# Spectral filter and two MLPs on one core: conversions, folds, mixing's weight parts and last low parts given other places

## Chip, core and metric

The kernel runs on one core of one Trainium2 chip. The metric is the device time of the program in microseconds (us) on that core, as the median of three runs. Durations of single instructions and stages come from one profiled execution of the program.

Engines are named as in the profile: PE is TensorE's matmuls and PEld its weight loads, DVE is VectorE, ACT is ScalarE, POOL is GpSimd, SP is SyncE, which issues the loads. A line number such as L865 is a line of the kernel's file.

## The reference

What is computed: a real FFT along the sequence, a complex 256x256 mixing with bias and a soft threshold, the inverse FFT, and then two MLPs of width 2048. The weights come in float64, x in float32.

```python
# x: (2, 3008, 256)
X = np.fft.rfft(x, axis=1)
Yr = Xr @ w_r - Xi @ w_i + b_r
Yi = Xr @ w_i + Xi @ w_r + b_i
Yr = np.sign(Yr) * np.maximum(np.abs(Yr) - 0.01, 0.0)      # Yi the same
y = np.fft.irfft(Yr + 1j * Yi, n=3008, axis=1)
# twice, on 6016 tokens, with w_in (256, 2048), w_out (2048, 256)
h = x @ w_in
g = h * (1.0 / (1.0 + np.exp(-1.702 * h)))                 # second MLP: 1.0 for 1.702
x = g @ w_out
```

## The kernel before

**Stages.** The transforms are matmuls with constant matrices. All regions have a hand-written order: an engine runs its instructions as the Python code issues them, and an instruction whose input or buffer isn't ready holds up everything behind it on that engine.

*Forward.* Sixteen groups (q, b, t): q is the half of the samples, b the batch, t the kind of output. Symmetric samples are folded first on VectorE. `halves` (L308) makes half-sums of a loaded tile, and `one` folds them once more, with L340, and for some pairs with L349, into the tiles xf. `fold(g)` does both for a group, and runs three groups ahead of its matmuls (L384, L398, L416). `fwd_evac` empties the banks of the group before: copies on ScalarE (L441, L445), and sums and differences on VectorE (L431, called from L451 to L457).

*Mixing.* Twelve units (b, p, j), the "mids", of 25 matmuls each from the third on (L565 and one of bias, L568) and 9 before (L562). From the third mid on, a float32 product is three matmuls of a high and a low part: hi·hi, hi·lo, lo·hi. Data: xh is a copy on ScalarE (L504); xl is made by a ScalarE product with -1 (L500) and a DMA that adds x to it (L501), issued on POOL's queue. Weights: wh is a ScalarE copy (L546), wl a VectorE difference (L547). `mid_post` (L575 to L586) and `mid_fold` (L598 to L605) do bias threshold and folds behind the matmuls, one mid late.

*Inverse.* Sixteen steps: matmuls at L384 (out of `inv_mm`), `inv_post` (L690 to L715, the differences again at L431), `inv_out` (L745 to L749). Its results yt stay on the chip.

*MLPs.* Six blocks of 1024 tokens (the last has 896), each with eight groups, and a group is a pair of column chunks of w_in. `group` forms its products X, Y, Z at L865 by a scheme with seven instead of eight block products: copies on ScalarE at L884, L900, L902, sums on VectorE at L886, L910, L913. The gate is two ScalarE steps, the activation L868 and the cast L870 of its high part; L875 makes the low part, on POOL or VectorE. The second product (L837) takes the gate's parts one group late (`out_next`). `hook(h)` is called at six places in a group, and adds other work there.

**Weight conversion.** Float64 weights arrive as pairs of 32-bit words in one buffer, raw64 (one buffer, loads issued by SP at L162, L163 or L166). A conversion is: L175 on ScalarE, which writes the tile cv_c (one buffer); five VectorE steps L180 to L184, which `pump` takes out of the list `fill`; and L185, an accumulating DMA on POOL's queue that adds cv_c to the tile cv_a, followed by the load of the next raw. `place_in` and `place_out` then split cv_a into high and low parts: sums L213 to L216 on VectorE, high parts L109 on ScalarE, low parts L110 on POOL or VectorE, or in mode "D" (L105 to L107) by the accumulating DMA. `tick` (forward) and `window(1, ())` (mixing, inverse, MLP) start a conversion.

Where they start is in CFG: 'tf' lists forward groups, 'tm' mids, 'ti' steps of the inverse. In the first MLP block 'kb' gives the number for each group. The conversions of its groups 0, 1 and 2 are called A, B and C here (parts out 3, 4 and 5); the next one is D. A sits at hook 4 of group 0, the others at hook 1 of their group. Hook 3 of the group after places what was converted, through `window(0, done, True)`.

Within a group the hooks stand in this order on ScalarE:

```python
884        nc.scalar.copy(y1, X)
887        hook(1)
893            g11 = gate(0, 0, y1)
900        nc.scalar.copy(y2, Z)
902        nc.scalar.copy(y3, X)
905        hook(3)
911        g22 = gate(1, 1, y2)
915        g12 = gate(0, 1, y3)
917        hook(4)
922        rest(nc.gpsimd, *gate(1, 0, y4, X))
```

(Hook 2 stands between L893 and L900.) The two lines of the hook that the change touches are L989 and L990.

Of the kernel before, what the change touches and what calls it, by code (L numbers as in the profile page):

```python
# [56 lines left out]
def spectral_mlp_kernel(ctx, tc, xin, mfwd, minv, wc, bias, w_in1, w_out1, w_in2, w_out2, outT):  # L57
# [4 lines left out]
    def N(k):  # L62
        return CFG.get(k, NUM[k])
# [1089 lines left out]
```

## Time and profile before

| what | us | share of the span |
|---|---|---|
| median of three runs (1172.51 to 1173.91) | 1173.24 | |
| profiled execution, its time | 1174.34 | |
| profiled execution, span | 1172.5 | |
| TensorE busy | 1150.7 | 98% |
| ScalarE busy | 772.5 | 66% |
| VectorE busy | 634.6 | 54% |
| POOL busy | 490.5 | 42% |
| moved by DMA | 66.65 MB | |

The mean granted clock of TensorE is 0.997 of full speed (full is 2.4 GHz). The span runs from the first to the last recorded instruction; the program's time has some 2 us more around it. Busy shares are means over stages: a share near 100% says that an engine can hardly be given less idle time, not that it never waits. The forward stage takes up the first 65 us, mixing goes on to about 133, the inverse to 185, and the rest is the two MLPs.

### The profile page before, as it was taken

How to read it: one execution, taken by the hardware profiler on the slowest of the kernel's cores; microseconds unless marked ns; L12 is line 12 of the kernel's file. 1: busy time of each engine (PE TensorE's matmuls, PEld its weight loads, DVE VectorE, ACT ScalarE, POOL GpSimd, SP SyncE). 2: the span in 40 equal slices, each digit the busy share in tenths (PEclk: the TensorE clock that was granted, in tenths of full speed). 3: DMA queues.
4: the chain of work that ended last, by engine and by line, in shares of the span. 5: the costliest groups of instructions: out<-in, count | busy, mean ns of one | idle time of the engine just before them, and what ended most of it. 6: DMA issues, size and time to landing. Idle time of an engine off the chain costs nothing.

```text
span 1172.5 us, 14601 instructions
## 1 busy us (share of the span) xinstructions
PE 1150.7 (98%) x5086; PEld 948.0 (81%) x5086; DVE 634.6 (54%) x1001; ACT 772.5 (66%) x1440; POOL 490.5 (42%) x418
## 2 busy tenths in 40 slices
PE   9999997999999999999999999999999999999998
PEld 6767865777888888888889978888888888888897
DVE  7778895676457465574573552442532623523522
ACT  2467455768667667677677776676766765866755
POOL 0255353444444444444446755343333333433333
PEclk9999999899999999999999999999999999999999
DMA  8566785421221121121220100010000000000000
GB/s 294 162 115 128 205 132 107 108 55 37 72 63 34 48 72 37 36 72 37 63 63 19 55 19 18 0 37 1 1 37 1 18 19 1 37 1 1 36 1 32
DMA packets 38268, 66.65 MB, mean 57 GB/s; under 512 B 3505, under 2 KB 15153, under 8 KB 38194
## 3 DMA queue, kind: packets, MB, share of 16 engines
q1 hardware_dynamic: 26306, 45.90, 11.9%
q0 software_dynamic: 11888, 19.82, 9.8%
q8 instruction: 40, 0.66, 0.2%
q14 instruction: 34, 0.28, 0.1%
HBM read 35.53 MB, written 10.35 MB: 39 GB/s over the span
## 4 chain that ended last, share of the span: by engine, by line
PE 81%; DVE 6%; ACT 4%; DMA 4%; issue 3%; POOL 1%; SPq 0%; DVEq 0%; ACTq 0%; POOLq 0%
PE o L837 40%; PE x L865 36%; PE psi L384 3%; DMA cv_a<-cv_c 2%; ACT yt L868 1%; DMA xl<-xt 1%; PE psf L384 1%; PE psf L416 1%; DMA raw<-in_x 1%; DVE cv_a L182 1%; ACT xh L504 0%; ACT xl L500 0%; DMA xr<-in_x 0%; ACT x L774 0%; ACT yt L884 0%
## 5 line engine op out<-in xcount | busy, mean ns | idle before, releaser
L875 POOL TENSOR_TENSOR g<-yt,g 128x512 fp32r<-128x512 f32 (+1 forms) x282 | 363.0, 1299 | 497.8 <-PE x L865 320.6
L837 PE MATMUL o<-g,wo 128*128 128x512 f32 (+1 forms) x2304 | 561.4, 386 | 0.6 <-DMA wo<-cv_a 0.6
L865 PE MATMUL x<-x,wi 128*128 128x512 f32 (+1 forms) x2016 | 500.8, 387 | 11.5 <-ACT yt L902 9.3
L837 PEld LDWEIGHTS o<-g,wo 128*128 128x128 f32 x2304 | 433.3, 188 | 82.0 <-DMA wo<-cv_a 1.0
L865 PEld LDWEIGHTS x<-x,wi 128*128 128x128 f32 x2016 | 377.6, 188 | 90.0 <-ACT yt L902 12.8
L868 ACT ACTIVATE yt<-yt 128x512 f32<-128x512 f32 (+1 forms) x288 | 179.2, 622 | 255.2 <-DVE yt L910 206.2
L870 ACT CAST g<-yt 128x512 fp32r<-128x512 f32 (+1 forms) x384 | 235.2, 612 | 12.2
L910 DVE TENSOR_TENSOR yt<-yt,x 128x512 f32<-128x512 f32 (+1 forms) x96 | 64.8, 675 | 217.5 <-PE x L865 216.9
L886 DVE TENSOR_TENSOR yt<-yt,x 128x512 f32<-128x512 f32 (+1 forms) x96 | 64.9, 676 | 166.7 <-ACT yt L884 166.4
L875 DVE TENSOR_TENSOR g<-yt,g 128x512 fp32r<-128x512 f32 (+1 forms) x102 | 70.2, 688 | 71.9 <-ACT g L870 71.0
L185 POOL DMA_DIRECT2D cv_a<-cv_c x32 | 28.1, 877 | 121.1 <-DVE cv_c L184 94.4
L913 DVE TENSOR_TENSOR yt<-yt,x 128x512 f32<-128x512 f32 (+1 forms) x96 | 64.8, 675 | 0.6 <-PE x L865 0.6
L781 DVE TENSOR_TENSOR x<-yt,x 128x512 fp32r<-128x512 f32 (+1 forms) x44 | 46.1, 1049 | 29.7 <-ACT x L774 29.7
L868 ACT ACTIVATE yt<-x 128x512 f32<-128x512 f32 (+1 forms) x96 | 56.1, 584 | 1.3 <-PE x L865 1.3
L884 ACT COPY yt<-x 128x512 f32<-128x512 f32 (+1 forms) x96 | 54.7, 570 | 2.4 <-issue 2.4
L902 ACT COPY yt<-x 128x512 f32<-128x512 f32 (+1 forms) x96 | 55.7, 580 | 0.1
L900 ACT COPY yt<-x 128x512 f32<-128x512 f32 (+1 forms) x96 | 54.8, 571 | 0.8 <-PE x L865 0.8
L384 PE MATMUL psi<-m,f 128*128 128x376 f32 (+3 forms) x208 | 50.2, 396 | 1.0 <-DVE rt L431 1.0
L384 PEld LDWEIGHTS psi<-m,f 128*128 128x128 f32 x208 | 36.5, 190 | 13.2 <-DVE rt L431 1.6
L175 ACT ACTIVATE cv_c<-raw 128x512 f32<-128x512 f32 x32 | 21.5, 673 | 22.6 <-DMA cv_a<-cv_c 18.2
L384 PE MATMUL psf<-m,xf 128*128 128x190 f32 (+2 forms) x176 | 36.1, 366 | 0.0
L565 PE MATMUL psm<-wh,xl 128*128 128x512 f32 x88 | 34.6, 393 | 1.1 <-DMA xl<-xt 1.0
(123 smaller groups left out, 853.5 us busy)
## 6 DMA issues: line engine op xcount, KB each, us to landing
raw<-in_wi SPq DMA_DIRECT2D x32, 256.0 KB, 3.6
cv_a<-cv_c POOLq DMA_DIRECT2D x32, 256.0 KB, 5.0
raw<-in_wo SPq DMA_DIRECT2D x16, 512.0 KB, 3.9
xl<-xt POOLq DMA_DIRECT2D x22, 256.0 KB, 5.5
out_t<-yt SPq DMA_DIRECT2D x20, 256.0 KB, 2.1
raw<-in_x SPq DMA_DIRECT2D x9, 512.0 KB, 5.6
m<-in_mi SPq DMA_DIRECT2D x4, 564.0 KB, 8.8
w_in<-cv_a SPq DMA_DIRECT2D x8, 256.0 KB, 2.0
```

Source lines behind the costliest of these rows:

```text
L384: nc.tensor.matmul(ps, hi[:, c : c + P], m[:, k, :w], start=i == 0, stop=i == last)
L837: nc.tensor.matmul(acc[h, mm], st, mv, start=first and k == 0, stop=last and k == 2)
L865: nc.tensor.matmul(ps, st, mv, start=first and m == 0, stop=m == 2, skip_group_check=True)
L868: nc.scalar.activation(g, g if src is None else src, func)
L870: nc.scalar.copy(gh, g)
L875: eng.tensor_sub(gl, g, r32(gh))
L884: nc.scalar.copy(y1, X)
L886: nc.vector.tensor_add(y1, y1, Y)
L900: nc.scalar.copy(y2, Z)
L902: nc.scalar.copy(y3, X)
L910: nc.vector.tensor_add(y2, y2, X)
L913: nc.vector.tensor_add(y3, y3, Z)
```

## The change

Seven edits, all of order, place or engine; the arithmetic is the same.

1. Forward: the third conversion tick goes from group 13 to group 14 ('tf').
2. Mixing: conversions start at mids 2, 5, 8, 10 instead of 1, 4, 7, 10 ('tm').
3. Inverse: the low parts L110 of weight part 4 go from VectorE to POOL.
4. `fold`: for groups with t = 0 behind the first, each half-sum is followed at once by the fold that reads it, instead of all half-sums first.
5. `xsplit`: the low parts of the last mid are made by POOL (tensor_sub) right behind their high parts, instead of a ScalarE product and an accumulating DMA each.
6. Start of mixing: wh and wl are issued ahead of the last `fwd_evac`.
7. MLP: B goes from hook 1 to hook 4 of group 1, C from hook 1 to hook 2 of group 2; A and the later ones stay.

```diff
--- before.py
+++ after.py
@@ -8,7 +8,7 @@
 
-CFG = {
...
-'tf': [6, 10, 13], 'tm': [1, 4, 7, 10],
...
+CFG = {
...
+'tf': [6, 10, 14], 'tm': [2, 5, 8, 10],
...
 
@@ -247,7 +247,7 @@
     def window(k, done, now=False):
         for u, a in done:
             if u[0] == "in":
-                sums, puts = place_in(u[1], u[2], a, (nc.vector if u[2] == NPR // 2 else "D") if modes[0] else E('pil', u[2]), sums_tmp)
+                sums, puts = place_in(u[1], u[2], a, (nc.gpsimd if u[2] == NPR // 2 else "D") if modes[0] else E('pil', u[2]), sums_tmp)
                 if now:
                     for f in (puts[0], *sums, puts[1]):
                         f()
@@ -313,12 +313,10 @@
         q, b, t = groups[g]
 
         cs, pair = t % 2, []
-        if t == 0 and g:
-            for j in range(NJ):
+        for j in range(NJ):
+            if t == 0:
                 halves(q, b, j, 0)
-        for j in range(NJ):
             if g == 0:
-                halves(q, b, j, 0)
                 one(0, j, pair)
                 halves(q, b, j, 1)
                 load_raw()
@@ -493,6 +491,8 @@
             return
         b, p, j = mids[i]
         k = (i - N('n32')) % 4
+        if part and i == len(mids) - 1:
+            return
         for cs in range(2):
             x = xt[b, p, j, cs].rearrange("p q m c -> p (q m c)")
             if part:
@@ -502,6 +502,10 @@
             else:
                 t = lo_p[1].tile([P, 512], F32R, tag="hi", name="xh")
                 nc.scalar.copy(t, x)
+                if i == len(mids) - 1:
+                    lo = lo_p[bool(k)].tile([P, 512], F32R, tag="lo", name="xl", bufs=6 if k else 2)
+                    nc.gpsimd.tensor_sub(lo, x, r32(t))
+                    xsp[b, p, j, cs, 1] = lo[:, :].rearrange("p (q m c) -> p q m c", q=2, m=2)
             xsp[b, p, j, cs, part] = t[:, :].rearrange("p (q m c) -> p q m c", q=2, m=2)
 
     first = fwd_first()
@@ -542,9 +546,9 @@
     lo_p.append(opened("nh", "left", N('nhb')))
     wh = wh_p.tile([P, 2, 3 * D], F32R, name="wh")
     wl = wh_p.tile([P, 2, 3 * D], F32R, name="wl")
-    fwd_evac(*prev)
     nc.scalar.copy(wh, wc_s)
     nc.vector.tensor_sub(wl, wc_s, r32(wh))
+    fwd_evac(*prev)
 
     def mid_mm(i):
         b, p, j = mids[i]
@@ -986,7 +990,7 @@
             if h == 3:
                 window(0, done, True)
                 done[:] = []
-            if h == (1 if at else 4):
+            if h == {0: 4, 1: 4, 2: 2}.get(at, 1):
                 window(k, ())
             if h in (2, 3):
                 moved(h)
```

## Rows read from the trace of the kernel before

**Rows 1.** TensorE's waits, whole span: us in total, times, longest.
```profile
PE x L865 <- ACT yt L902: 9.3, 8, 6.3
PE psf L416 <- DVE xf L340: 1.7, 1, 1.7
...
PE psm L565 <- DMA xl<-xt: 1.0, 1, 1.0
```

**Rows 2.** timeline of TensorE, MLP's groups 1 and 2: start, us, instruction [idle <-releaser].
```profile
196.77 2.92 PE L837 MATMUL o<-g,wo 128*128 128x512 f32 x12
205.95 2.93 PE L865 MATMUL x<-x,wi 128*128 128x512 f32 x6 [6.26 <-ACT yt L902]
...
211.24 2.27 PE L865 MATMUL x<-x,wi 128*128 128x512 f32 x9
```

**Rows 3.** stretches: length, busy us of PE, PEld, DVE, ACT, POOL; PEclk, DMA, GB/s.
```profile
199.00:204.50 5.50, 0.69 (x4) 0.23 (x2) 0.68 (x2) 1.37 (x3) 1.23 (x1) 1.00 0.57 140
204.50:206.00 1.50, 0.05 (x1) 0.05 (x1) 1.40 (x4) 1.40 (x3) 0.00 (x0) 0.50 0.00 0
300.00:400.00 100.00, 99.76 (x441) 82.27 (x440) 56.36 (x78) 67.76 (x120) 42.16 (x34) 1.00 0.19 50
```

**Rows 4.** timeline of ScalarE, MLP's groups 0 and 1: conversions A and B.
```profile
193.62 0.66 ACT L175 ACTIVATE cv_c<-raw 128x512 f32<-128x512 f32 x1
...
203.10 0.66 ACT L175 ACTIVATE cv_c<-raw 128x512 f32<-128x512 f32 x1 [7.20 <-DMA cv_a<-cv_c]
```

**Rows 5.** line L185, stretches 193:200, 105:106, 112:120 and 236:240.
```profile
DMA to landing us min/median/max: 5.0/5.0/5.0
...
DMA to landing us min/median/max: 4.5/4.5/4.5
...
L185 POOL DMA_DIRECT2D cv_a<-cv_c x1: 877/877/877, 117.1 to 117.1; - x1
...
DMA to landing us min/median/max: 8.4/8.4/8.4
...
DMA to landing us min/median/max: 6.1/6.1/6.1
```

**Rows 6.** timeline of VectorE, MLP's group 1.
```profile
197.66 0.68 DVE L886 TENSOR_TENSOR yt<-yt,x 128x512 f32<-128x512 f32 x1
```

**Rows 7.** page, costliest groups: busy us, mean ns of one, idle before, releaser.
```profile
L868 ACT ACTIVATE yt<-yt 128x512 f32<-128x512 f32 (+1 forms) x288 | 179.2, 622 | 255.2 <-DVE yt L910 206.2
...
L902 ACT COPY yt<-x 128x512 f32<-128x512 f32 (+1 forms) x96 | 55.7, 580 | 0.1
```

**Rows 8.** timeline of VectorE, forward stage.
```profile
15.08 0.69 DVE L308 TENSOR_TENSOR keep<-xr 128x512 f32<-128x512 f32 x1 [0.59 <-DMA xr<-in_x]
...
26.39 2.43 DVE L340 TENSOR_TENSOR xf<-lv 128x256 f32<-128x256 f32 x7
...
32.77 0.76 DVE L349 TENSOR_TENSOR xf<-dd 128x256 f32<-128x256 f32 x2 [0.51 <-PE psf L384]
...
37.91 0.43 DVE L181 TENSOR_SCALAR cv_c<-cv_c 128x512 uint32<-128x512 uint32 x1
```

**Rows 9.** timeline of ScalarE, start of mixing.
```profile
65.00 0.47 ACT L445 COPY eo<-psf 128x376 f32<-128x376 f32 x1 [4.09 <-DVE xt L431]
```

**Rows 10.** timeline of TensorE, start of mixing.
```profile
67.42 0.50 PE L565 MATMUL psm<-wh,xh 128*128 128x512 f32 x1 [0.22 <-ACT xh L504]
68.69 0.50 PE L565 MATMUL psm<-wl,xh 128*128 128x512 f32 x1 [0.78 <-DVE wl L547]
```

**Rows 11.** timeline of VectorE, end of mixing and inverse.
```profile
148.66 0.55 DVE L110 TENSOR_TENSOR wi<-cv_a,wi 128x384 fp32r<-128x384 f32 x1
...
156.68 0.55 DVE L431 TENSOR_TENSOR rt<-psi,eo 128x376 f32<-128x376 f32 x1
```

**Rows 12.** timeline of ScalarE, mid 10.
```profile
125.52 0.67 ACT L175 ACTIVATE cv_c<-raw 128x512 f32<-128x512 f32 x1 [1.03 <-DMA cv_a<-cv_c]
```

**Rows 13.** timeline of VectorE, last ticks of the forward stage.
```profile
59.88 1.11 DVE L181 TENSOR_SCALAR cv_c<-cv_c 128x512 uint32<-128x512 uint32 x1
```

More of the change, by code (lines that the diff above doesn't have):

```diff
@@ L10 @@
 F32 = mybir.dt.float32
-CFG = {'lv0': 'V', 'lv': 'V', 'dd0': 'VPVVPPPPPVVP', 'dd': 'V', 'ths': 'VVVVPV', 'thf': 'VVVP', 'ivf': 'V', 'cva': 'P', 'pol': 'PPPP', 'pil': 'P', 'mvl': 'PVVP', 'xl': 'V', 'xse': 'V', 'gl': 'VPPPPPPP', 'tf': [6, 10, 13], 'tm': [1, 4, 7, 10], 'ml': [], 'pk': 6, 'ti': [3, 7], 'pi': 4, 'pl': [1, 4, 8, 10, 13], 'kb': [1, 1, 1, 1, 1, 1, 1, 0], 'kr': [0, 1, 0, 1, 0, 1, 1, 0], 'fa': 3, 'xp': [2, 4, 4, 5], 'xq': [1, 4, 1], 'xs': 4, 'xi': [7, 7, 9, 10, 10, 11, 8], 'xsi': 9, 'xo': (0, 1, 6, 2, 3, 4, 5), 'xd': (0, 1, 4, 6), 'ca': 4, 'tl': True, 'fwd': 'all', 'rest0': 'all', 'rest1': 'all', 'last1': 'all', 'inv': 'all', 'mid': 'all', 'last0': 'all', 'thm': 'A', 'gl0': 'PVPVVVPV', 'gl2': 'PPPPPPPP', 'gl3': 'PPPPPPPV', 'xl0': 'V', 'xl1': 'V', 'pre': 14, 'pre2': 0, 'yd': 6, 'lvb': 6, 'mlp': 'all', 'pr': 'V', 'pf': 'PV', 'eo': '0110', 'n32': 1, 'li': [8, 10, 11], 'lii': [0], 'xa': 4, 'nhb': 6, 'ddb': 6, 'mlp1': 'all', 'mlp2': 'all'}
+CFG = {'lv0': 'V', 'lv': 'V', 'dd0': 'VPVVPPPPPVVP', 'dd': 'V', 'ths': 'VVVVPV', 'thf': 'VVVP', 'ivf': 'V', 'cva': 'P', 'pol': 'PPPP', 'pil': 'P', 'mvl': 'PVVP', 'xl': 'V', 'xse': 'V', 'gl': 'VPPPPPPP', 'tf': [6, 10, 14], 'tm': [2, 5, 8, 10], 'ml': [], 'pk': 6, 'ti': [3, 7], 'pi': 4, 'pl': [1, 4, 8, 10, 13], 'kb': [1, 1, 1, 1, 1, 1, 1, 0], 'kr': [0, 1, 0, 1, 0, 1, 1, 0], 'fa': 3, 'xp': [2, 4, 4, 5], 'xq': [1, 4, 1], 'xs': 4, 'xi': [7, 7, 9, 10, 10, 11, 8], 'xsi': 9, 'xo': (0, 1, 6, 2, 3, 4, 5), 'xd': (0, 1, 4, 6), 'ca': 4, 'tl': True, 'fwd': 'all', 'rest0': 'all', 'rest1': 'all', 'last1': 'all', 'inv': 'all', 'mid': 'all', 'last0': 'all', 'thm': 'A', 'gl0': 'PVPVVVPV', 'gl2': 'PPPPPPPP', 'gl3': 'PPPPPPPV', 'xl0': 'V', 'xl1': 'V', 'pre': 14, 'pre2': 0, 'yd': 6, 'lvb': 6, 'mlp': 'all', 'pr': 'V', 'pf': 'PV', 'eo': '0110', 'n32': 1, 'li': [8, 10, 11], 'lii': [0], 'xa': 4, 'nhb': 6, 'ddb': 6, 'mlp1': 'all', 'mlp2': 'all'}
 NUM = dict(li=[5, 6, 7, 8], n32=2, pk=4, ydp=2, lii=[1, 3], xd=(), ml=[], pl=[], xo=range(7), pi=6, nhb=6, tf=[5, 9, 13], tm=[1, 3, 5, 7, 9, 11], ti=[0, 2, 4, 6, 8, 10, 12, 14, 14, 15, 15], kb=[2] * 8, kr=1, fa=3, fe=2, pm=0, nf=4, lvb=6, ddb=8, ivb=1, eob=1, fsb=6, f1=3, f2=0, fm=[7, 8, 9], fi=[1, 1, 2, 2], pre=13, pre2=1, yd=3, psh=0, ie=[12], xp=[1, 3, 4, 5], xq=[1, 2, 2], xs=5, nw=4, xi=[14, 14, 15, 15], xsi=13, rw=2, ca=4, cc=2, tb=1, tmn=1)
```

## The prediction

> **What bounds the kernel now.** Three views, in this order. The page's busy shares (the table above) give TensorE 98% of the span: moving work can win only what TensorE waits for, or runs at a lower clock. TensorE's waits [rows 1] then name the places: one of 6.3 us in the MLP, for the copy L902, one of 1.7 in the forward fold (xf) and one of 1.0 at the end of mixing (xl). Each lies in a stage that the change touches. Last the timelines around the long one. TensorE ends its work at 199.69 (196.77 + 2.92) and goes on at 205.95 [rows 2]. The granted clock is full until 204.5 and half, 1.2 GHz, after it [rows 3]: the 12 matmuls from 205.95 to 211.24 take 5.29 us [rows 2]. In a steady stretch one follows the other by 100 / 441 = 0.227 us [rows 3], so twelve would take 2.7. The place costs 6.3 + 2.5 = 8.8 us.
>
> Its cause stands in ScalarE's queue [rows 4]. Conversion A's L175 runs at 193.62; behind the copy L884 of group 1 comes conversion B's L175 (hook 1 of group 1). It writes cv_c, of which there is one, and A's accumulating transfer still reads it: B's L175 waits 7.20 us, to 203.10, and the gate, L900 and L902 queue behind it. From one L175 to the next takes 203.10 - 193.62 = 9.5 us at the least, 5.0 of it the transfer [rows 5].
>
> **MLP: B to hook 4 of group 1, C to hook 2 of group 2.** In group 1 no transfer is waited for any more. L886 still stands on VectorE behind A's five steps and starts at 197.66 [rows 6]; 0.7 for it, 1.2 for the gate (L868 and a cast of the same size) and 1.2 for L900 and L902 [rows 7] bring L902's end to 200.7, and TensorE, ready at about 199.4, waits 1.3. From there two matmul groups, L910 and two gates (0.7 + 0.6 + 2.4, [rows 6, 7]) put B's L175 at 204.4, after A has landed: no wait. But between hook 4 of group 1 and hook 2 of group 2 ScalarE has only a gate, L884 and a gate (about 3.5 us), and the turn-round is 9.5. C's L175 can't start before 213.8; L900 and L902 behind it end at 215.4. TensorE, 45 matmuls (10.2 us at 0.227) after 200.4, wants L902 at 210.6: it waits 4.8 us there. So the wait is not gone, it stands one group later: 1.3 + 4.8 against 6.3 us. B and C are now placed together in group 3 (two more ScalarE casts in one hook, 1.1 us), and the last matmuls of group 2 come late behind the gates: 0.7 more. D follows C by nearly a whole group, so its wait is covered. Idle time then gets 0.6 us worse, and what is won is the half clock, 2.5 us, if it stays full over 4.8 us. In the old wait it fell at 204.5, 4.8 us after the last matmul; I take it that it just stays: **-1.9 us**. If it falls, +0.6. Were the wait gone altogether, 8.8 - 2.0 = 6.8 us would be won: the lower end.
>
> **The fold.** For groups with t = 0 each half-sum is now followed by its fold. In group 2 the half-sums come one by one with their loads, the last of them at 15.08 [rows 8]. So the first folds fill these gaps instead of standing behind 15.08, and the 1.7 us wait goes. It comes back: TensorE is next late for group 5, whose last fold (26.39) closes a VectorE row without a gap since 15.08. Two folds of 0.35 (2.43 / 7) taken out of that row, and some 0.5 of bubbles between dependent steps added, leave 0.15 us. In group 8 the order hurts: the fold at 32.77 waits 0.51 us for TensorE [rows 8], and now a half-sum (0.6) that used to be ahead of it stands behind. The conversion that follows on VectorE comes 0.6 us later, and with it the chain of transfers to mixing.
>
> **Start of mixing.** The conversion tick goes from group 13 to 14, and wh, wl ahead of the last evacuation. The tick itself doesn't move, since its L175 waited for a landing; but VectorE now evacuates group 13 before it. L445 waited 4.09 us for that, at 65.00 [rows 9], and wh stood behind it. Now wh stands right behind the copy of group 14, at about 61. ScalarE, which then runs without a gap for some 10 us, carries 4.0 us into the stage, and wl comes some 2 us earlier. TensorE's matmul for wl starts 68.69 - 67.42 = 1.27 after the one ahead of it [rows 10], 1.0 more than 0.227; the shorter wait ahead (0.22) and slow restarts make it some 1.5, by estimate, and all of it goes.
>
> **Mixing, and who gains from it.** The four conversions go from mids 1, 4, 7, 10 to 2, 5, 8, 10; the low parts of the last mid go from ScalarE and two transfers to POOL, 1.3 us each. The stall for xl (a wait of 1.0 [rows 1], 1.5 with restarts, taken from the place of wl) goes too, and TensorE could leave mixing 3.0 us early. It can't keep that: banks for the second half of the inverse are freed by VectorE's L431 at 156.68 [rows 11], and from mid 10's L175 (125.52, which waits for the third conversion's landing) [rows 12] VectorE has next to no gap up to there. That landing decides. Its transfer, issued at 117.1, took 8.4 us [rows 5]. Now: 117.1 - 4.0 (start) + 0.6 (fold) + 5.7 (one mid later: 25 matmuls at 0.227) = 119.4. How long it takes there no row shows: 4.5 at the least, 8.4 at the most [rows 5]. I take 5.5, near the short end, as the two transfers for xl that followed it are gone and two of four matrix loads no longer fall on it. It lands at 124.9, 0.6 before 125.5; by the ends, 1.6 before or 2.3 after.
>
> **Weight part 4 to POOL.** VectorE loses two L110 of 0.55 from 148.66 on [rows 11], 1.1 us in that row. POOL is idle there but for issues. A VectorE step beside a POOL L110 stretches: L181 took 1.11 us instead of 0.43 [rows 8, 13]. The first new POOL step falls on the sums L213 to L216, I put 0.3 on that; the second falls on L714 and L715, which read PSUM. Gain 0.8, between -0.2 and 1.1. The Trainium skill (SBUF — State Buffer, section "SBUF: two separate sides") says that a GpSimd operation and a VectorE operation with two SBUF inputs take a port pair in turns, each for its whole length. L181 agrees. If that held for every step beside the two, the gain would be gone and the time some 0.8 us more.
>
> L431 so comes 0.6 + 0.8 = 1.4 us earlier, and TensorE with it: **-1.4 us**, of 3.0 that it could have had; behind it TensorE is bound by its own matmuls up to the MLP. With the ends: 2.7 won, or 2.5 lost (2.3 late, 0.2 lost).
>
> **Sum.** The profiled execution has a span of 1172.5 and a time of 1174.34; the median is 1173.24. The differences are worked out on the span and taken off the median: 1173.24 - 1.4 - 1.9 = 1169.9.
>
> **Rivals.** (a) The clock falls again in the 4.8 us wait of group 2: price 2.5, 1172.4, within 0.2%. For it speaks that the rows show the fall at just that length of idling. The Trainium skill (TensorE: Matmul & The Clock Gate, section "HAM oscillation — how this bites in real kernels") warns that idle gaps put the array back to half clock, again and again in one kernel; by that rule 1172.4 is the result. Against it: one fall is all that the rows hold, and the new wait is no longer than the idling that came before it.
> (b) TensorE keeps what it wins in mixing, because the landing is quick and VectorE keeps up: 1173.24 - 3.0 - 1.9 = 1168.3. Against it: the gapless row on VectorE.
> (c) The wait in group 2 is hidden: 1173.24 - 1.4 - 6.8 = 1165.0. It would need a turn-round of under 5 us, where 9.5 is the shortest seen.
> (d) Slower: accumulating transfers land late where other loads run beside them. In mixing, 8.4 us puts L431 1.5 later (2.3 - 0.8). In the MLP 6.1 instead of 5.0 (which another of block 0 took [rows 5]) makes the wait of group 2 5.9 and takes the clock with it: +1.7. Together 1176.4. It decides from about 7 us in mixing; before, a landing of 8.4 came with four matrix loads and two xl transfers, now half of that.
> (e) That an edit does nothing, as for the tick of group 14: covered by (a), 1172.4.
>
> **How the numbers follow.** Forecast 46%, (a) with (e) 27%, (b) 12%, (c) 4%, (d) 11%. The range leaves out (c) and most of (d): 1166.6 to 1174.2. A measurement of this kernel can tell about 0.2% (2.3 us) from no change, that is 1170.9 and 1175.6. The forecast's cases lie below 1170.9 mostly (0.40 of 0.46), (b) and (c) wholly; (a) is the same but for 0.02; of (d) 0.09 is slower: faster 0.58, same 0.33, slower 0.09.
>
> **What would show it.** Right: a wait of TensorE for L902 of about 4.8 us in group 2 (near 209 to 214) and one of about 1.3 in group 1, at a full clock; no wait for xf in group 2 but small ones up to group 5; no waits for wl and xl; a wait of 1.5 to 3 us in the first half of the inverse for L431, and TensorE at the MLP's first matmul 1 to 2 us earlier than before. Wrong: half clock after the new wait; ScalarE at mid 10 waiting more than 3 us for the landing; the first MLP matmul 3 us earlier or more, which would say that VectorE doesn't bound the inverse.

## Result and profile after

The changed kernel takes 1179.16 us (median of 5 runs, 1178.32 to 1180.14) where the kernel before takes 1173.37 beside it: a ratio of 1.0051, 95% interval 1.0037 to 1.0066. It is slower by 6 us, and the forecast had it 3.3 us faster. Its profiled execution has a time of 1179.16 and a span of 1177.4, against 1172.5 before. One execution each of three kernels below took far longer (e7 3906.59, e9 3792.0, e10 1278.03 us) and is left out of medians and ratios.

Code ahead of `xsplit` stands 2 lines higher in the changed kernel, and code behind it 4 lines lower: L902 is now L906, L865 is L869, L837 is L841, L565 is L569, L579 is L583, L431 is L429, L340 is L338. L500 and L504 keep their numbers.

Where the time went is first seen by stage, one profiled execution of each kernel. The table has the starts of TensorE's first matmul of mixing (psm), of the inverse (psi) and of the MLPs (x), from the timelines of both kernels, and the distances between them.

| | mixing starts | inverse starts | MLPs start | mixing | inverse | MLPs to the last matmul's start |
|---|---|---|---|---|---|---|
| before | 59.93 | 133.58 | 185.52 | 73.65 | 51.94 | 982.85 |
| after | 60.36 | 135.68 | 191.84 | 75.32 | 56.16 | 981.40 |

Mixing lost 1.7 us and the inverse 4.2; the MLPs are 1.4 shorter. So what the forecast had from the stages ahead of the MLP (-1.4) came with the other sign, at +5.9. The MLPs' 1.4 looks like most of the forecast (-1.9), but kernels with the same MLP code differ by as much from profile to profile (see e3).

TensorE's waits of the changed kernel (us in total, times, longest) name what is new there:

```profile
PE x L869 <- ACT yt L906: 8.7, 9, 4.6
PE psm L569 <- ACT xh L504: 2.9, 2, 2.0
PE psi L382 <- DVE rt L429: 2.7, 2, 1.5
PE psi L382 <- DVE sd L583: 1.8, 1, 1.8
```

Against [rows 1]: the waits of 1.7 for xf and 1.0 for xl's transfer are gone, as forecast, but mixing now waits 2.9 us for xh, which before was late by 0.2 at the most [rows 10], and the inverse 1.8 for sd and 2.7 for rt (before, 1.0 for rt). Who holds up xh stands in ScalarE's timeline (start, us, instruction, [idle before <-releaser]):

```profile
112.05 1.39 ACT L587 ACTIVATE th<-sd,neglam 128x512 f32<-128x512 f32 x2 [4.53 <-DVE sd L581]
...
118.18 0.66 ACT L175 ACTIVATE cv_c<-raw 128x512 f32<-128x512 f32 x1 [3.71 <-DMA cv_a<-cv_c]
...
121.37 1.12 ACT L504 CAST xh<-xt 128x512 fp32r<-128x512 f32 x2
...
132.61 0.67 ACT L175 ACTIVATE cv_c<-raw 128x512 f32<-128x512 f32 x1 [3.75 <-DMA cv_a<-cv_c]
```

The first of the two waits for xh (0.9, at 112.7) comes from VectorE: its five steps of the second conversion (107.4 to 110.1) keep sd late, and L587 ahead of xh waits 4.53 for that. The second (2.04, at 119.6) comes from L175: the third conversion's (mid 8) waits 3.71 us for the second's transfer, and xh, at 121.37, stands behind it. The fourth's (mid 10) waits 3.75 us for the third's transfer, and starts at 132.61, 7.1 us later than its counterpart of [rows 12]. The accumulating transfers they wait for, line L185 in the stretches 110:112 and 125:126:

```profile
L185 POOL DMA_DIRECT2D cv_a<-cv_c x1: 877/877/877, 110.8 to 110.8; - x1
...
DMA to landing us min/median/max: 7.4/7.4/7.4
...
L185 POOL DMA_DIRECT2D cv_a<-cv_c x1: 877/877/877, 125.2 to 125.2; - x1
...
DMA to landing us min/median/max: 7.4/7.4/7.4
```

Both take 7.4 us. Before, the second conversion's transfer, of 105.4, took 4.5 [rows 5].

The clock falls twice. Stretches of the changed kernel (columns as in [rows 3]):

```profile
122.00:123.00 1.00, 0.98 (x4) 0.85 (x5) 0.93 (x3) 0.97 (x2) 0.00 (x0) 0.97 0.00 0
123.00:126.00 3.00, 3.00 (x8) 2.35 (x8) 2.93 (x6) 0.00 (x0) 0.85 (x2) 0.50 0.10 11
126.00:127.00 1.00, 1.00 (x5) 0.78 (x5) 1.00 (x4) 0.56 (x1) 1.00 (x2) 0.83 0.80 252
222.00:225.00 3.00, 2.90 (x7) 2.33 (x8) 2.90 (x6) 1.08 (x3) 0.78 (x2) 0.50 0.00 0
225.00:226.00 1.00, 1.00 (x6) 0.78 (x5) 0.96 (x2) 0.60 (x1) 0.98 (x2) 0.83 0.95 228
```

The half clock from just before 123 to 126.3 follows the 2.0 us wait for xh and makes mixing some 1.7 us longer; the other follows the new wait in the MLP:

```profile
207.00 1.66 PE L869 MATMUL x<-x,wi 128*128 128x512 f32 x6 [1.04 <-ACT yt L906]
...
214.63 2.88 PE L841 MATMUL o<-g,wo 128*128 128x512 f32 x12
222.10 2.93 PE L869 MATMUL x<-x,wi 128*128 128x512 f32 x6 [4.58 <-ACT yt L906]
```

That is rival (a)'s fall, after a wait of 4.58 us (forecast: 4.8) behind one of 1.04 in group 1 (forecast: 1.3).

### The profile page after: what moved, and what is told of

Its sections match the earlier page's. It is cut to its first block, busy times and chain, and to the rows that moved or that the text cites. A ratio compares the mean times of both kernels' runs of the same rounds, so it can differ in the third digit from the quotient of the medians.

```text
span 1177.4 us, 14595 instructions
## 1 busy us (share of the span) xinstructions
PE 1152.0 (98%) x5086; PEld 948.7 (81%) x5086; DVE 636.8 (54%) x999; ACT 772.3 (66%) x1438; POOL 494.1 (42%) x420
## 4 chain that ended last, share of the span: by engine, by line
PE 77%; DVE 5%; ACT 3%; issue 3%; DMA 1%; POOL 1%; DVEq 0%; POOLq 0%; ACTq 0%
PE o L841 39%; PE x L869 35%; PE psi L382 3%; ACT yt L872 1%; DMA cv_a<-cv_c 1%; DVE yt L890 0%; DVE cv_a L182 0%; ACT x L778 0%; ACT yt L888 0%; DVE th L590 0%; ACT g L874 0%; DVE cv_c L180 0%; DVE yt L914 0%; DVE tmp L213 0%; POOL g L879 0%
## 5 line engine op out<-in xcount | busy, mean ns | idle before, releaser
L841 PE MATMUL o<-g,wo 128*128 128x512 f32 (+1 forms) x2304 | 560.3, 385 | 0.5 <-DMA wo<-cv_a 0.5
L869 PE MATMUL x<-x,wi 128*128 128x512 f32 (+1 forms) x2016 | 500.8, 387 | 10.9 <-ACT yt L906 8.7
L841 PEld LDWEIGHTS o<-g,wo 128*128 128x128 f32 x2304 | 432.8, 188 | 81.7 <-DMA wo<-cv_a 1.0
L869 PEld LDWEIGHTS x<-x,wi 128*128 128x128 f32 x2016 | 377.3, 188 | 89.7 <-ACT yt L906 12.7
L914 DVE TENSOR_TENSOR yt<-yt,x 128x512 f32<-128x512 f32 (+1 forms) x96 | 64.8, 675 | 217.1 <-PE x L869 216.7
L185 POOL DMA_DIRECT2D cv_a<-cv_c x32 | 28.1, 878 | 125.4 <-DVE cv_c L184 93.0
L906 ACT COPY yt<-x 128x512 f32<-128x512 f32 (+1 forms) x96 | 55.8, 582 | 0.1
L569 PE MATMUL psm<-wh,xh 128*128 128x512 f32 x88 | 35.5, 404 | 2.9 <-ACT xh L504 2.9
L382 PEld LDWEIGHTS psf<-m,xf 128*128 128x128 f32 x176 | 29.6, 190 | 8.2 <-ACT xt L439 1.2
```

Source lines behind the costliest of these rows:

```text
L382: nc.tensor.matmul(ps, hi[:, c : c + P], m[:, k, :w], start=i == 0, stop=i == last)
L841: nc.tensor.matmul(acc[h, mm], st, mv, start=first and k == 0, stop=last and k == 2)
L869: nc.tensor.matmul(ps, st, mv, start=first and m == 0, stop=m == 2, skip_group_check=True)
L914: nc.vector.tensor_add(y2, y2, X)
```

## Experiments

Ratios are to the kernel before, run beside each, with 95% intervals; 1% is 11.7 us. Each batch had its own runs of the kernel before, with medians from 1173.37 to 1174.09. Stage lengths come from TensorE's timelines, as in the table above, one profile each: mixing took 73.65, 72.72 and 72.73 us in three kernels with the same mixing (before, e3, e7), so a difference of 1 us in a stage is not read as an effect. The edits below show of CFG's line only the entry that differs.

| kernel | median us | ratio | mixing | inverse | MLPs |
|---|---|---|---|---|---|
| before | 1173.37 to 1174.09 | 1 | 73.65 | 51.94 | 982.85 |
| after | 1179.16 | 1.0051 (1.0037 to 1.0066) | 75.32 | 56.16 | 981.40 |
| e1_tm_back | 1169.10 | 0.9958 (0.9944 to 0.9972) | 69.62 | 50.69 | 981.53 |
| e2_tm_alone | 1183.93 | 1.0083 (1.0070 to 1.0096) | 75.46 | 58.31 | 982.29 |
| e3_hook_alone | 1173.43 | 0.9998 (0.9989 to 1.0007) | 72.72 | 51.83 | 982.93 |
| e4_load_later | 1178.05 | 1.0033 (1.0020 to 1.0045) | 72.36 | 56.88 | 982.48 |
| e5_fold_alone | 1172.02 | 0.9990 (0.9981 to 0.9998) | 73.42 | 51.58 | 982.05 |
| e6_start_alone | 1169.56 | 0.9968 (0.9956 to 0.9980) | 69.61 | 50.93 | 982.14 |
| e7_pool_alone | 1172.99 | 0.9996 (0.9987 to 1.0005) | 72.73 | 50.74 | 981.79 |
| e8_xl_alone | 1174.32 | 1.0007 (0.9999 to 1.0016) | 70.36 | 53.26 | 983.13 |
| e9_mid11 | 1176.15 | 1.0017 (1.0008 to 1.0026) | 74.86 | 52.36 | 982.55 |
| e10_mid11_load9 | 1174.02 | 0.9999 (0.9990 to 1.0008) | 72.83 | 53.11 | 982.66 |
| e11_8_10 | 1172.26 | 0.9983 (0.9974 to 0.9992) | 69.62 | 54.24 | 982.35 |
| e12_8_11 | 1168.89 | 0.9965 (0.9952 to 0.9977) | 70.63 | 52.20 | 981.92 |
| h_4332 | 1170.00 | 0.9971 (0.9960 to 0.9982) | 69.62 | 50.68 | 983.91 |
| h_3332 | 1170.16 | 0.9970 (0.9958 to 0.9981) | 69.62 | 50.69 | 983.31 |
| b13 | 1159.50 | 0.9881 (0.9867 to 0.9894) | 69.62 | 50.68 | 973.19 |
| b14 | 1159.82 | 0.9884 (0.9870 to 0.9897) | 69.62 | 50.84 | 973.72 |

Mixing is never shorter than 69.6 and the inverse never shorter than 50.7: in e1 TensorE waits for nothing in either, so these are its own work in the two stages. The kernel before stood 4.0 and 1.3 us above them.

### Is it mixing's new places?

Theory: the loss is the four new places of mixing's conversions ('tm'), through the waiting L175. Rival: another of the seven edits, or the places only together with the others.

e1_tm_back, on the changed kernel:

```diff
-'tm': [2, 5, 8, 10]
+'tm': [1, 4, 7, 10]
```

> The changed kernel with mixing's conversions back at mids 1, 4, 7, 10; the other six edits stay. Theory: the loss is the third conversion's L175, at mid 8, held for 3.7 us by the second conversion's transfer, which now runs beside the matrix load of mid 8 (7.4 us to landing, 4.5 before). Then TensorE's two waits for xh (0.9 and 2.0 us), the half clock behind them and the longer waits in the inverse go, and the time falls below the kernel before, by the 1.4 us that the MLP gives or more: 1169.5 to 1172. Rival: the new places of mixing's weights and of the last low parts, or the fold, delay mixing by themselves: then it stays above 1175 and waits for xh remain.

Measured: 1169.10, ratio 0.9958. ScalarE's timeline has the second to fourth L175 almost without waits:

```profile
85.66 0.66 ACT L175 ACTIVATE cv_c<-raw 128x512 f32<-128x512 f32 x1
...
105.25 0.69 ACT L175 ACTIVATE cv_c<-raw 128x512 f32<-128x512 f32 x1
...
119.86 0.67 ACT L175 ACTIVATE cv_c<-raw 128x512 f32<-128x512 f32 x1 [0.20 <-DMA cv_a<-cv_c]
```

e2_tm_alone, on the kernel before:

```diff
-'tm': [1, 4, 7, 10]
+'tm': [2, 5, 8, 10]
```

> The kernel before with only mixing's conversions moved to mids 2, 5, 8, 10. Theory: this edit alone makes the loss; the second conversion's transfer is issued at about 111, beside the matrix load of mid 8, lands after 118, and L175 of mid 8 waits some 3.5 us: 1177 to 1181. Rival: the loss needs the other edits with it (POOL's steps, an earlier start): then within 2 us of before.

Measured: 1183.93, ratio 1.0083. The loss is 3 us more than the most expected. TensorE waits 3.24 us for sd in the inverse here, and the clock is at half from 143.2 to 146.6 behind that. The same two waits are in ScalarE's timeline:

```profile
119.52 0.66 ACT L175 ACTIVATE cv_c<-raw 128x512 f32<-128x512 f32 x1 [2.59 <-DMA cv_a<-cv_c]
...
133.91 0.67 ACT L175 ACTIVATE cv_c<-raw 128x512 f32<-128x512 f32 x1 [3.69 <-DMA cv_a<-cv_c]
```

What follows: the places cost 0.0083 alone and 1.0051 - 0.9958 = 0.0093 beside the others, 10 to 11 us either way. The other six edits together win 0.0042, 4.9 us. This edit alone turned the sign.

### Why the new places cost that much

Two causes were put to the test: the load of the inverse's matrices at mid 8 (line L137; 'li' lists its mids), which now runs beside the second conversion's transfer, and the distance of two mids between the third and the fourth conversion.

e4_load_later, on the changed kernel:

```diff
-'li': [8, 10, 11]
+'li': [9, 10, 11]
```

> The changed kernel with the matrix load of mid 8 moved to mid 9, nothing else. Theory (the matrix load makes the transfer land late): the second conversion's transfer lands in about 4.5 us again, L175 at mid 8 waits under 1 us, waits for xh are under 0.5 us in all, and the time is 1171 to 1175. Rival (the steps ahead of the transfer are late by themselves, or its own two low-part transfers slow it): L175 at mid 8 still waits over 2.5 us and the time stays above 1176.5.

Measured: 1178.05, ratio 1.0033, 0.0018 (2.1 us) less than the changed kernel. The mechanism is as expected at mid 8: with the load away, the transfer issued at 111.8 lands in 4.4 us and L175 waits 0.69. But the loads, now four together at 123.17, meet the next transfer, of 123.2: it takes 8.2 us, and mid 10's L175 waits 4.47 (line L185 in 111:112 and 123:124, then ScalarE's timeline):

```profile
L185 POOL DMA_DIRECT2D cv_a<-cv_c x1: 875/875/875, 111.8 to 111.8; - x1
...
DMA to landing us min/median/max: 4.4/4.4/4.4
...
L185 POOL DMA_DIRECT2D cv_a<-cv_c x1: 877/877/877, 123.2 to 123.2; - x1
...
DMA to landing us min/median/max: 8.2/8.2/8.2
```

```profile
116.19 0.68 ACT L175 ACTIVATE cv_c<-raw 128x512 f32<-128x512 f32 x1 [0.69 <-DMA cv_a<-cv_c]
...
131.42 0.67 ACT L175 ACTIVATE cv_c<-raw 128x512 f32<-128x512 f32 x1 [4.47 <-DMA cv_a<-cv_c]
```

So the expected time (1171 to 1175) was wrong. The move gives back a fifth of the loss, as the collision went on to the next transfer instead of away; what a kernel without any collision would take, no run shows.

e9_mid11 and e10_mid11_load9, on the changed kernel (e9 has the first edit, e10 both):

```diff
-'tm': [2, 5, 8, 10]
+'tm': [2, 5, 8, 11]
-'li': [8, 10, 11]
+'li': [9, 10, 11]
```

> The changed kernel with the fourth conversion of mixing at mid 11 instead of 10 (places 2, 5, 8, 11). Theory: a conversion's turn-round in mixing is 7.0 us from L175 to its transfer's issue and 4.4 to 8.4 more to landing, 11.4 to 15.4 in all, and two mids are 11.4 us, three are 17.0. Then L175 of the fourth waits under 1 us instead of 3.75, and about half of the 10 us that the new places cost comes back: 1173 to 1176. Rival: one mid later only moves the wait, and VectorE's steps of the fourth conversion fall into the inverse: no better than 1178.

> The changed kernel with places 2, 5, 8, 11 and the matrix load of mid 8 moved to mid 9. Theory: now neither the third nor the fourth L175 waits more than 1 us, TensorE has no wait for xh over 0.5 us, and the time comes near to the one with places 1, 4, 7, 10 (1169.1): 1169 to 1172. Rival: the places are late for the inverse anyway, whose waits for VectorE stay over 2 us: above 1174.

Measured: 1.0017 and 0.9999. The fourth at mid 11 is worth 0.0034 (4.0 us), its L175 waits 1.12 and 0.94 us. Both causes together are worth 0.0052 (6.1 us), which is the sum of what each is worth by itself. But e10 isn't at e1's 0.9958: 0.0041 (4.8 us) stay, in 3.2 us of mixing and 2.4 of the inverse. Its third L175 still waits 1.40 us. The last two runs on this keep the first two places of before.

e11_8_10 and e12_8_11, on the changed kernel:

```diff
-'tm': [2, 5, 8, 10]
+'tm': [1, 4, 8, 10]    (e11)
+'tm': [1, 4, 8, 11]    (e12)
```

> The changed kernel with mixing's places at mids 1, 4, 8, 10: third and fourth two mids apart, the first two as before. Theory of spacing: the third L175 waits for nothing, the fourth waits some 4 us for the third's transfer (7.0 + 7.5 to 8.4 against 11.4), TensorE waits for xh there: 3 to 5 us over the 1169.1 of places 1, 4, 7, 10: 1172 to 1174.5. Rival, lateness alone: as with 1, 4, 8, 11.

> The changed kernel with mixing's places at mids 1, 4, 8, 11: three or more mids apart, but the last two one mid later than before. Theory of spacing: no L175 waits over 1 us, 1169 to 1171. Rival, lateness: VectorE's steps of the third and fourth conversion fall on the end of mixing and the first steps of the inverse, TensorE waits there 2 us or more: 1172 to 1174.

Measured: 0.9983 and 0.9965. In e11 the fourth L175 waits 3.85 us, and TensorE's waits behind it come in the inverse (54.24, 3.6 above e1's); the time is 2.9 us above e1's. In e12 it waits 1.14 (under 1 was expected), and the time is 0.0007 above e1, within the intervals (its profiled execution took 1170.74, so its stages in the table look longer than that).

```profile
110.17 0.66 ACT L175 ACTIVATE cv_c<-raw 128x512 f32<-128x512 f32 x1
...
124.70 0.66 ACT L175 ACTIVATE cv_c<-raw 128x512 f32<-128x512 f32 x1 [3.85 <-DMA cv_a<-cv_c]
```

```profile
113.03 0.66 ACT L175 ACTIVATE cv_c<-raw 128x512 f32<-128x512 f32 x1
...
127.49 0.68 ACT L175 ACTIVATE cv_c<-raw 128x512 f32<-128x512 f32 x1 [1.14 <-DMA cv_a<-cv_c]
```

What follows: for the last two places spacing is the cause, and that they come later in mixing is not. The turn-rounds (from an L175 to the landing of its transfer) show where each pair is too close. From an L175 to the issue of its transfer it takes 7.0 us where VectorE has nothing to place first (118.18 to 125.15 in the changed kernel, 110.17 to 117.15 in e11), and, for the second conversion, 14.9 to 16.4, as VectorE places a weight part first (90.49 to 105.42 before, 94.35 to 110.75 after). To landing it takes 4.3 to 5.1 us more without a matrix load beside it and 7.0 to 8.6 with one.

| | distance to the next L175, its wait taken off | turn-round | its wait |
|---|---|---|---|
| before, second to third (mids 4, 7) | 110.09 - 90.49 = 19.6 | 14.9 + 4.5 = 19.4 | 0 |
| after, second to third (5, 8) | 118.18 - 3.71 - 94.35 = 20.1 | 16.4 + 7.4 = 23.8 | 3.71 |
| e4, second to third (5, 8) | 116.19 - 0.69 - 95.37 = 20.1 | 16.4 + 4.4 = 20.8 | 0.69 |
| after, third to fourth (8, 10) | 132.61 - 3.75 - 118.18 = 10.7 | 7.0 + 7.4 = 14.4 | 3.75 |
| e12, third to fourth (8, 11) | 127.49 - 1.14 - 113.03 = 13.3 | 7.0 + 7.5 = 14.5 | 1.14 |

That the wait is what the turn-round has over the distance is so by construction, as L175 starts on the landing; what the rows tell is which of the two moved. Before, 0.2 us were to spare for the second to the third; the change left that distance alone and made its turn-round 4.4 us longer, and it made the distance of the third to the fourth shorter than any turn-round of the table. What remains between e10 and e12, some 4 us, goes with the first two places, the only edit between them beside the matrix load of mid 8; in e10 the third L175 still waits 1.40 us, and TensorE waits 0.9 for xh as in the changed kernel. By which of these the first two places cost that much is not shown.

Why a late L175 costs time far behind it shows when its start in mid 10, which is the landing of the third conversion's transfer, is set beside the start of the MLPs:

| | L175 of mid 10 | MLPs start | distance |
|---|---|---|---|
| before | 125.52 | 185.52 | 60.00 |
| e2 | 133.91 | 193.87 | 59.96 |
| e3 | 124.35 | 184.36 | 60.01 |
| e5 | 125.69 | 185.69 | 60.00 |
| e6 | 122.04 | 182.04 | 60.00 |
| e8 | 124.30 | 184.26 | 59.96 |
| e7, part 4 on POOL | 125.00 | 184.24 | 59.24 |
| after, part 4 on POOL | 132.61 | 191.84 | 59.23 |
| e4, part 4 on POOL | 131.42 | 190.63 | 59.21 |
| e11, part 4 on POOL | 124.70 | 183.94 | 59.24 |

In all ten this landing sets the MLPs' start to within 0.1 us, whatever TensorE waited for before it; with the fourth conversion at mid 11 (e9, e10, e12; landings at 132.28, 130.29 and 127.49) the distance is 55.4. In e1 and in three of the four versions built on it below, the distance is up to 1.2 us longer: there the MLPs start 120.3 us after mixing, TensorE's own work in the two stages. So the half clock in mixing added nothing: the changed kernel has the same distance as e11, which ran mixing and inverse at a full clock.

### The other edits alone

Each on the kernel before; the edits are those of the diff ahead of the prediction: e3 has the hook line, e5 `fold`, e6 'tf' and the place of wh and wl, e7 nc.gpsimd in `window`, e8 `xsplit`.

```diff
-            if h == (1 if at else 4):                    (e3)
+            if h == {0: 4, 1: 4, 2: 2}.get(at, 1):
```

> The kernel before with only the MLP's conversions B and C moved (hook 4 of group 1, hook 2 of group 2). Theory: the wait of 6.3 us becomes one of about 1.2 in group 1 and one of about 4.7 in group 2, the clock falls again but for some 3 us instead of 5.4: 1.4 us won, 1171.5 to 1172.3. Rival, that the MLP gains only by what came before it in the changed kernel (its start was 6.3 us later): no gain, 1173 to 1174.

Measured: 0.9998. TensorE's timeline has the two waits of the forecast, and the stretch behind the second the half clock:

```profile
199.50 1.66 PE L865 MATMUL x<-x,wi 128*128 128x512 f32 x6 [1.04 <-ACT yt L902]
...
214.78 2.93 PE L865 MATMUL x<-x,wi 128*128 128x512 f32 x6 [4.79 <-ACT yt L902]
```

```profile
214.00:219.00 5.00, 4.21 (x10) 3.35 (x11) 4.52 (x8) 2.65 (x6) 1.76 (x2) 0.50 0.22 54
219.00:220.00 1.00, 1.00 (x3) 0.79 (x3) 0.53 (x1) 0.97 (x3) 0.00 (x0) 0.50 0.88 243
220.00:221.00 1.00, 1.00 (x5) 0.76 (x4) 1.00 (x2) 0.55 (x1) 0.36 (x1) 0.78 1.14 232
```

Here 12 matmuls follow the first at a half-clock distance of 0.43 us, in the changed kernel and in e1 six, in e2 eight, in e9 and e10 eleven, behind waits of 4.6 to 4.8 us (6.3 in e2). Six matmuls at half clock are 6 * (0.43 - 0.227) = 1.2 us; that is most of the difference between the MLPs of e3 (982.93) and of e1 (981.53). The rival's time came true, and the expectation of 1.4 had been read from one profile. The rival's reason is not borne out: in e1 the MLPs start earlier than here, and are the shorter. Over the eight kernels with this edit the MLPs take 981.40 to 982.93 (mean 982.2), over the six with the old hooks 981.79 to 983.13 (before, e2, e5 to e8; mean 982.4): the edit wins some 0.1 us by that, an estimate, and the 1.4 lies within the spread. What sets when the clock comes back, no run isolates.

> The kernel before with only the fold's new order. The forecast's step: the 1.7 us wait for xf in group 2 goes and comes back as small waits up to group 5, and group 8's conversion starts 0.6 us later: within 0.5 us of before. Rival: VectorE keeps what it wins, and mixing starts 1.5 us earlier.

Measured: 0.9990 (0.9981 to 0.9998): a small gain, a little more than forecast. The 1.7 us wait for xf is gone, and four of 0.2 to 0.9, 1.9 in all, stand in its place; the profile (1173.69) doesn't show the gain, its MLPs start at 185.69 (before 185.52).

> The kernel before with only edits 1 and 6 (tick at group 14; wh and wl ahead of the last evacuation). TensorE's wait for wl (0.8, some 1.5 with restarts) goes. Theory now: mixing is paced by TensorE's matmuls and by the conversions together, and the conversions of mids 4, 7 and 10 have no slack before their landings; an earlier start moves all of them, and 1.5 us stay: 1171.5 to 1172.5. Rival of the forecast: VectorE's row in front of the inverse swallows it: no change.

Measured: 0.9968, 3.8 us, the largest of the six and more than twice the 1.5 that was expected. Mixing is at TensorE's own 69.6 us: not only wl's wait goes, but xl's too. The third conversion's transfer lands at 122.0 instead of 125.5 [rows 12], and the MLPs start 3.5 us earlier:

```profile
122.04 0.67 ACT L175 ACTIVATE cv_c<-raw 128x512 f32<-128x512 f32 x1 [0.84 <-DMA cv_a<-cv_c]
```

> The kernel before with only weight part 4's low parts on POOL. The forecast's step: 0.8 us (between -0.2 and 1.1) off VectorE's row in the inverse, and the wait of 1.0 for rt gets shorter by as much: 1172.4. Rival (POOL and VectorE stretch each other's steps): no gain or 0.8 us more.

Measured: 0.9996; the time can't be told from no change. The trace has the wait for rt gone, and the distance from mid 10's L175 to the MLPs is 59.24 instead of 60.00: the 0.8 of the forecast.

> The kernel before with only the last mid's low parts on POOL. The wait of 1.0 us for xl goes, and two accumulating transfers beside the third conversion's: its 8.4 us to landing gets shorter, to 6 to 7, and mid 10's L175 (1.0 us of waiting) isn't held: 1.5 us or more at the end of mixing, of which the inverse keeps 1 to 2: 1171 to 1172.5. Rival: the landing stays above 8 us, as the matrix load beside it sets it; VectorE's row swallows the rest: no change.

Measured: 1.0007, no change, as the rival had it. In the trace mixing is 3.3 us shorter than before (2.4 than in e3), and the inverse is 1.3 longer, with a longer wait for rt. The landing at 124.30 is no earlier than e3's, 124.35, so TensorE can't keep what it wins:

```profile
PE psi L384 <- DVE rt L431: 1.6, 1, 1.6
```

The third transfer still took 8.0 us to land (116.25 to 124.28) without the two transfers for xl behind it, so these don't set it.

### A version without the MLP's stop

With mixing's places back, the largest idle time left is the MLP's: 1.0 + 4.7 us and the half clock. Two ways to spread its conversions were run on e1 (h_4332 and h_3332), and two that move the first of them into the inverse, with all others at hook 1 as before the change (b13 and b14).

```diff
-            if h == {0: 4, 1: 4, 2: 2}.get(at, 1):
+            if h == {0: 4, 1: 3, 2: 3, 3: 2}.get(at, 1):    (h_4332)
+            if h == {0: 3, 1: 3, 2: 3, 3: 2}.get(at, 1):    (h_3332)
```

> The changed kernel with mixing's places back at 1, 4, 7, 10 and the MLP's conversions at hook 4 of group 0, hook 3 of groups 1 and 2, hook 2 of group 3. Theory: the 8 us that lie between hook 4 and hook 1 of one group are given up in three steps of at most 2.5 us, each turn-round of 9.5 us then nearly fits, no wait of TensorE in block 0 is over 2 us and the clock stays full: 3 to 4 us under the 1169.1 of the run with mixing's places back: 1165 to 1167. Rival: at hook 3 the waiting L175 holds VectorE's five steps and L914 behind them, and TensorE waits there instead: within 1 us of 1169.

> As the run with hooks 4, 3, 3, 2, but group 0 also converts at hook 3. Theory: the first conversion's steps no longer stand ahead of L890 in group 1 (a wait of TensorE of 1.0 there) and the second gets 2.5 us more: 1 to 2 us better, 1164 to 1166. Rival: group 0 is short of TensorE's work (it has no second product), so hook 3's steps hold its own sums: no better than hook 4, or worse by up to 1.5.

Measured: 0.9971 and 0.9970, no better than e1. The rival was right. L175 at hook 3 holds VectorE's five steps, and L914 stands behind them; TensorE waits for that instead of for L906, and the clock falls behind the longest of these waits (3.5 and 4.1 us) as well:

```profile
PE x L869 <- DVE yt L914: 7.4, 5, 3.5
PE x L869 <- ACT yt L906: 4.2, 8, 1.0
```

```diff
-'ti': [3, 7], 'kb': [1, 1, 1, 1, 1, 1, 1, 0],
+'ti': [3, 7, 13], 'kb': [0, 1, 1, 1, 1, 1, 1, 0],    (b14: 14)
-            if h == {0: 4, 1: 4, 2: 2}.get(at, 1):
+            if h == (1 if at else 4):
```

> The changed kernel with mixing's places back at 1, 4, 7, 10, and the first conversion of the MLP at step 13 of the inverse instead of hook 4 of group 0; the MLP's others at hook 1 of their groups, as before the change. Theory: no two conversions of the MLP are closer than one group of 10.2 us, a turn-round of 9.5 fits, the waits of 1.2 and 4.8 us and the half clock (1.6) go, VectorE's five steps (3 us) fall into its gaps at the end of the inverse: 5 to 7 us under 1169.1: 1162 to 1164. Rival: the steps hold the sums at the end of the inverse or the first group's sums, and 3 us are given back: 1165 to 1167.

> As b13, with the first conversion at step 14 of the inverse. Theory: within 1 us of b13. Rival: its steps run into the first group of the MLP and hold L890 there: 1 to 3 us slower than b13.

Measured: 1159.50 and 1159.82, ratios 0.9881 and 0.9884: 14 us faster than the kernel before and 20 than the changed one, and 2.5 us better than the best expected (1162). In b13's timeline of ScalarE the conversions stand a group apart (13.4, 10.4 and 9.6 us), and one waits 0.92 us; TensorE's longest wait for L906 is 0.9, and its clock stays full:

```profile
176.59 0.68 ACT L175 ACTIVATE cv_c<-raw 128x512 f32<-128x512 f32 x1
...
190.00 0.68 ACT L175 ACTIVATE cv_c<-raw 128x512 f32<-128x512 f32 x1
...
200.38 0.66 ACT L175 ACTIVATE cv_c<-raw 128x512 f32<-128x512 f32 x1 [0.92 <-DMA cv_a<-cv_c]
...
209.96 0.67 ACT L175 ACTIVATE cv_c<-raw 128x512 f32<-128x512 f32 x1
```

```profile
PE x L869 <- ACT yt L906: 3.0, 7, 0.9
```

```profile
196.00:215.00 19.00, 19.00 (x86) 15.73 (x85) 13.43 (x22) 15.03 (x27) 7.94 (x7) 1.00 0.46 98
```

The MLPs take 973.2 instead of 981.5 us, and the inverse is no longer (50.7): four of the five steps stand at 177.3 to 179.4, behind a gap of 2.57 us in VectorE's row, and TensorE's waits in the inverse and in the MLP's first group are those of e1 (none, and 0.7 and 0.2).

## Why the prediction was wrong, step by step

- **What bounds the kernel; the long wait.** Right. ScalarE's L175 behind a transfer that still reads cv_c is what stops TensorE, in the MLP before the change and in mixing after it.
- **MLP, -1.9.** The waits were right to within 0.3 us: 1.04 and 4.58 (forecast 1.3 and 4.8), one group later. The gain was not: it was to be the half clock, "if it stays full", and the clock fell, as in rival (a), in the profile of every kernel that has the new wait. The fall was not always worth the 2.5 us taken for it either; it lasted 6 to 12 matmuls. The edit alone won nothing by time, some 0.1 by the means of the MLPs' lengths; that the changed kernel's profile has 1.4 is luck.
- **The fold, 0.** Nearly right: 1.2 us won, alone (0.9990), at the edge of the interval. The wait came back as smaller ones, as forecast.
- **Start of mixing, 1.5, kept in part.** Too small. Alone the edit wins 3.8 us, as the whole chain of conversions moves by 3.5 us with it, up to the landing at 122.0, and the MLPs' start by the same 3.5. The 4.0 us that ScalarE carries into mixing were seen; that they are worth nearly their whole length by themselves was not.
- **Mixing: the step that failed is the time of the third conversion's landing.** "That landing decides" was right, and so was its price: it came at 132.6, 7.1 us after 125.5, and 7.1 less the 0.8 of weight part 4 is 6.3, just what the MLPs' start lost (191.84 - 185.52). But the forecast had it at 124.9, and it came 7.7 later. The sum was 117.1 - 4.0 + 0.6 + 5.7 = 119.4 for the issue of the third conversion's transfer. It was issued at 125.2. Of the 5.8 us between, 3.71 are the wait of the third L175 for the second conversion's transfer. That transfer moved by a mid as well, and so fell on the matrix load of mid 8: it took 7.4 us where 4.5 had been read. The working asked only whether the third landing holds the fourth L175, and never whether the second holds the third. The other 2.1 are the head start: without the wait, L175 would have run at 118.18 - 3.71 = 114.47, and one mid after its old place (110.09 + 5.7) is 115.8, so the chain had 1.3 us left of the 3.4 that the sum gave it. About 1 us of these 2.1 goes with the places: in e2, without the head start, L175 without its wait would have run at 119.52 - 2.59 = 116.93, 1.1 after 115.8. Why the rest was lost no run isolates; with the old places the head start stayed (third issue at 112.3 in e1, 4.8 before 117.1).
- **The transfer's length.** 5.5 us were taken, between 4.5 and 8.4; it took 7.4, the other 1.9 of the 7.7. One reason for the short end was the two transfers for xl; e8 shows that they don't set it (8.0 us without them). The other was that only two of four matrix loads were left beside it. They were enough (issued from 125.09): two make the second conversion's transfer 7.4 us long, and without them it takes 4.4 (e4).
- **VectorE's gapless row in front of the inverse.** Right: the distance from the landing to the MLPs is fixed. When mixing ends early and the landing doesn't move, TensorE waits (e8: 1.6 us for rt); in e6 the landing moved along, and TensorE kept all it won.
- **Weight part 4 to POOL, 0.8.** Right by the traces: the distance above is 59.2 with it and 60.0 without; by time (0.9996) it can't be told. The exclusive port pair of the Trainium skill (SBUF — State Buffer, section "SBUF: two separate sides") didn't turn it into a loss. One step shows it: beside POOL's first step in e7 (1.00 us at 144.52), L213 took 0.55 us instead of 0.28, about the 0.3 that was taken off; L714 and L715 beside the second kept their 0.54 and 0.55. L181, which the prediction names as agreeing, reads one tile; the row with two SBUF inputs is L182 behind it, 1.64 us at 61.02 instead of 0.69.
- **Rivals.** (d) came nearest: slower, by late landings, mixing hit first. It had 11% and 1176.4. But that number is luck in part: by its own rule a transfer of 7.4 us costs some 0.5 in mixing, and the loss came from the transfer's issue, 5.8 us late by the wait of the third L175 and the shrunk head start; its other half, a longer wait in the MLP (5.9), didn't come (4.58). (a)'s fall of the clock came as well. Two of the prediction's three signs of being wrong were there: the half clock, and 3.75 us of waiting at mid 10. What no rival held is the wait of the third L175, at mid 8.

## What to carry to other kernels

Where a chain of steps shares one buffer, its period is the longest turn-round (steps, then the transfer at its slowest), not the mean. Before places of such steps are moved, write that period beside each distance between neighbours, for every pair and not only for the one that is late now: here two of three neighbours were too close; the places cost 10 us, and mending these two pairs gave 6 of them back (e10). Then look for the one event that the next stage starts from: here, in ten kernels, the MLPs' start followed one landing at a fixed distance, and what TensorE won elsewhere in mixing it lost again waiting for that. When a wait only moves from one place to the next, there is one step too many in the stretch, and moving one to a stage with slack (here 3 us of VectorE's work into the end of the inverse, with the others back at hook 1, worth 8.3 us in the MLP) does more than spreading them.

## What the runs showed of the hardware

- The accumulating transfers of mixing's conversions (256 KB) that were issued in mixing landed in 4.3 to 5.1 us without matrix loads beside them, and in 7.0 to 8.6 with the first of two or more issued within 0.5 us; the same one went from 7.4 to 4.4 when only the load was moved (e4).
- After a wait of TensorE of the same length (4.6 to 4.8 us) the granted clock stayed at half for 6 to 12 matmuls of 0.43 us, by the kernel. In mixing it fell in the changed kernel after 2.04 us of waiting, with 0.90 us of waiting 8 us ahead of it, and in e2 it stayed full after 1.99 us with 1.53 us 8 us ahead. In the inverse it fell after 2.57 us (e4) and 3.24 us (e2). So a wait of 2 us isn't free of a fall, and doesn't always bring one.
